# First-layer weights in column halves, the second half prepared during the second batch

## The chip, the core and the metric

The kernel runs on one core of a Trainium2 chip. The core has five engines with separate instruction streams: TensorE (PE, matrix products; its weight loads are listed as PEld), VectorE (DVE), ScalarE (ACT), GpSimd (POOL) and SyncE (SP), which here only issues DMA transfers. Each engine works through its own instructions in the order in which they were written and stops at the first whose inputs or buffers are not ready. The metric is the device time of one execution in microseconds (us).

## The reference

Attention over 8 batches of 8 heads, 576 positions and 64 channels, in which every score that lies more than tau below the maximum of its row is dropped, followed by two dense layers over all 4608 tokens. The numbers are float32 outside the kernel.

```python
scores = scale * np.matmul(q, k.transpose(0, 1, 3, 2))
thresh = np.max(scores, axis=-1, keepdims=True) - tau
scores = np.where(scores >= thresh, scores, -1000000000.0)
attn = softmax(scores)                     # written out in the reference
x = (attn @ v), heads side by side         # 4608 x 512
h = x @ w_in                               # 512 x 2048
out = (h - np.tanh(h)) @ w_out             # 2048 x 512
```

`w_in` and `w_out` hold 4 MB each in float32; the kernel keeps both in on-chip memory as bfloat16 (`w_in_sb`, `w_out_sb`).

## The kernel before

**Tiles.** Two heads form a pair; there are 32 pairs, four to a batch. A pair has nine tiles of 128 query rows: four for each head, and one that the last 64 rows of both heads share. That makes 288 tiles. The tile's scores are a 128 x 576 block (`psS`), written by PE from `kT` and `kS` (the pair's keys, transposed, and the same with halves swapped) and `qT`.

**What a pair needs first.** `load` brings k, q and v from memory over SP's queue (`kraw`, `qraw`, `vraw`). `split` on POOL makes a high and a low float16 part of k and of q (L184, L187, L188: three instructions each). `turn` transposes them, on PE with a copy by DVE (L258), or for the queries of every second pair from pair 9 on with a DMA transpose (L247); for keys POOL then makes `kS` (L264, two instructions). `split_v` on POOL casts the values (L216, L220, L221).

**A tile's way.** PE makes the scores; DVE scales them and takes their row maxima (L336, `sc`); once for two tiles DVE makes the threshold `nb` (L348); ACT applies the cut (`kink`, L363, giving `z`); `z` is transposed, for pairs 0 to 5 on PE (L382), from pair 6 on by a DMA transpose for two tiles at a time (L370, `zT`), issued on SP; ACT takes the exponential (`weights`, L391 after PE, L399 after the DMA, both giving `pT`); PE multiplies with the values (`attend`, L420, L427, L438); DVE divides (`norm`).

**The dense layers.** When a batch's four pairs are done, its 512 main tokens go through both layers in small steps put between the tiles of the next batch: `hidden` (L493, one of 16 column blocks of `w_in_sb`), tanh on ACT (L506), the subtraction on DVE (L512), `project` (L519, with `w_out_sb`). The last batch's share and the remaining rows run after the last tile.

**The order of work** is written out by hand. The main loop runs over s from -8; in step s the scores of tile s + 8 are made. I number steps by that tile, t = s + 8. So pair p's first scores come in step 9p. `PREP` and `plan` say in which step a pair's preparations are issued: `split` of k in step 9p - 8 and of q in 9p - 7 (for the odd pairs from 9 on in 9p - 10 and 9p - 9), the keys' `turn` in 9p - 5 (from pair 5 on in 9p - 6 or 9p - 3), `split_v` in 9p - 4, the loads in 9p - 16 to 9p - 14. In a tile's step t, ACT does the cut of tile t - 3, and the exponential of tile t - 4 in the first batch and of tile t - 8 later.

**The weights** come in 16 pieces of 512 KB, eight of `w_in` and then eight of `w_out`. A piece is loaded by SP into one of two float32 buffers `wt` (L638 for `w_in`, L634 for `w_out`), and POOL casts it into its place (L626). `w_when` lists the steps. In each listed step, after everything else of that step, the piece loaded at the previous listed step is cast and the next one is loaded. So SP stops at a load until POOL has cast the piece but one before it, and everything behind the load in SP's queue stops with it. Before, the loads stand in steps 3, 7, ..., 63 and the casts in steps 7, 11, ..., 67. A piece of `w_in` covers 128 of its 512 rows and half of its 2048 columns, pieces 0 and 1 being the left and the right half of the first rows, and so on.

The first `hidden` step stands in t = 49, the first that reads the right half of the columns (block 8) in t = 63, and the first that reads `w_out_sb` (L519) in t = 76.

Of the kernel before, what the change touches and what calls it, by code (L numbers as in the profile page):

```python
# [18 lines left out]
def kernel(  # L19
# [594 lines left out]
    def w_pieces():  # L614
        for w, sb, n in ((moe_w_in, w_in_sb, DM_C), (moe_w_out, w_out_sb, DF_C)):
            flat = sb.rearrange("p c n -> p (c n)")
            cols = n * w.shape[1] // 8
            src = w.rearrange("(c p) n -> p c n", p=P)
            for i in range(8):
                yield flat, src, i, cols, w.shape[1]  # L620

    loaded = []
# [50 lines left out]
    for t in ("k", "q", "v"):  # L673
        load(1, t)
    pieces = w_pieces()
    w_when = [4 * i + 3 for i in range(17)]

    todo, stage = [], 0
    fold = const.tile([P, 64], BF16, name="fold")
# [125 lines left out]
```

## Time and profile before

| | before |
|---|---|
| median of six runs | 534.15 us (533.56 to 535.31) |
| the profiled execution's own time | 534.04 us |
| its span in the profile | 532.1 us, so 1.9 us lie around it |
| PE busy | 505.9 us (95%) |
| DVE, ACT, POOL busy | 423.8, 436.2, 290.2 us |
| one cast of a weight piece (L626, POOL) | 1.039 us, 16 of them |
| one load of a weight piece, issue to landing | 4.5 us (`w_in`), 4.3 us (`w_out`) in the median |
| one DMA transpose of `z`, issue to landing | 3.6 us in the median, 6.3 us at most |

Times in the profile count from the start of the span. A line of the timeline gives start and duration, the engine, the line of the code, the operation with output <- input, and in brackets how long the engine stood idle before it and what ended that. In the rows by stretch each engine's busy time and its number of instructions are followed by the granted clock of PE, the mean busy share of the 16 DMA engines and the rate that they moved. The busy share of an engine over the whole span says little here: the first 60 us, with attention alone, are limited by other things than the 400 us in which both parts run side by side.

### The profile page before, as it was taken

What the parts mean: (1) busy time and instruction counts of PE and PEld (TensorE: products, weight loads), DVE (VectorE), ACT (ScalarE), POOL (GpSimd) and SP (SyncE); (2) the same over time, 40 slices, a digit from 0 to 9 for tenths busy, and PEclk for the clock granted to TensorE, in tenths of its full rate; (3) what the DMA queues carried; (4) which work ended last, traced back from release to release, by engine and by line L of the source; (5) the groups of instructions that cost most, each with busy time, mean ns of one, the idle gap of its engine ahead of it and who ended that gap; (6) DMA issues with size and microseconds to landing.
All of it is one profiled execution on the core that took longest, in us unless ns stands there. A gap on an engine that the chain in (4) does not pass through costs nothing.

```text
span 532.1 us, 12733 instructions
## 1 busy us (share of the span) xinstructions
PE 505.9 (95%) x4584; PEld 289.2 (54%) x4651; DVE 423.8 (80%) x1184; ACT 436.2 (82%) x617; POOL 290.2 (55%) x390
## 2 busy tenths in 40 slices
PE   8988899999999999999999999999999999999997
PEld 4666566554556565555555555655555555444444
DVE  5888878988988998898889998899889887554440
ACT  5999899998898998989888989898889899543330
POOL 7999987774745757475737574575747530000000
PEclk9999999999999999999999999999999999999999
DMA  7554557989997999899897999899989985401113
GB/s 212 176 187 147 173 160 193 186 167 187 171 201 148 190 179 211 173 169 211 188 186 156 198 187 194 147 193 186 205 169 177 200 155 110 105 22 39 39 41 79
DMA packets 202686, 85.31 MB, mean 160 GB/s; under 512 B 170240, under 2 KB 195072, under 8 KB 202624
## 3 DMA queue, kind: packets, MB, share of 16 engines
q1 hardware_dynamic: 202032, 84.08, 74.6%
q8 instruction: 36, 0.59, 0.4%
q10 hardware_dynamic: 592, 0.43, 0.3%
q14 instruction: 26, 0.21, 0.1%
HBM read 36.70 MB, written 9.44 MB: 87 GB/s over the span
## 4 chain that ended last, share of the span: by engine, by line
PE 63%; ACT 11%; POOL 8%; DVE 7%; issue 6%; DMA 4%; SPq 1%; POOLq 0%; ACTq 0%; DVEq 0%
PE psY L519 20%; PE psH L493 16%; PE psS L326 14%; ACT z L363 5%; PE psO L427 3%; ACT pT L399 3%; DMA zT<-z 3%; PE psHt L493 3%; ACT th L506 2%; POOL kS L264 2%; PE ps_k L235 2%; PE psS L317 2%; DVE sc L336 2%; DVE g L512 2%; POOL w_in_sb L626 1%
## 5 line engine op out<-in xcount | busy, mean ns | idle before, releaser
L336 DVE TENSOR_SCALAR_CACHE_REDUCE sc<-psS 128x576 f32<-128x576 f32 x288 | 214.4, 753 | 36.3 <-PE psS L326 22.7
L363 ACT ACTIVATE z<-sc,nb 128x576 bf16<-128x576 f32 x288 | 217.0, 771 | 29.1 <-DVE nb L348 27.1
L519 PE MATMUL psY<-w_out_sb,g 128*128 128x512 bf16 (+1 forms) x571 | 141.7, 373 | 2.4 <-issue 0.8
L264 POOL COPY kS<-kT 64x1152 f16<-64x1152 f16 x62 | 70.9, 1144 | 124.2 <-DVE nb L348 122.6
L399 ACT ACTIVATE pT<-zT 128x1152 f16<-128x1152 bf16 x117 | 135.1, 1155 | 3.8 <-DMA zT<-z 3.8
L493 PE MATMUL psH<-xT,w_in_sb 128*128 128x512 bf16 x436 | 114.1, 379 | 4.4 <-DVE g L512 2.3
L326 PE MATMUL psS<-kT,qT 128*128 128x512 f16 (+1 forms) x512 | 104.3, 285 | 4.6 <-DVE sc L336 2.0
L326 PEld LDWEIGHTS <-qT 128*128 128x128 f16 x1024 | 74.4, 97 | 59.9 <-issue 6.4
L512 DVE SCALAR_TENSOR_TENSOR g<-th,psH 128x512 bf16<-128x512 f32 x128 | 87.5, 684 | 21.3 <-ACT th L506 20.9
L326 PE MATMUL psS<-kS,qT 128*128 128x512 f16 x496 | 101.3, 286 | 0.3 <-POOL kS L264 0.3
L506 ACT ACTIVATE th<-psH 128x512 f32<-128x512 f32 x128 | 74.8, 584 | 23.3 <-PE psH L493 22.8
L519 PEld LDWEIGHTS <-g 128*128 128x128 bf16 x592 | 51.0, 98 | 56.8 <-issue 2.4
L493 PEld LDWEIGHTS <-w_in_sb 128*128 128x128 bf16 x576 | 49.1, 98 | 57.0 <-issue 4.7
L427 PE MATMUL psO<-vb,pT 128*128 128x65 bf16 x1024 | 53.3, 194 | 0.0
L427 PEld LDWEIGHTS <-pT 128*128 128x128 f16 x1024 | 44.2, 98 | 9.4
L188 POOL TENSOR_TENSOR qhl<-qraw,qhl 128x576 f16<-128x576 f32 x31 | 39.7, 1281 | 2.6
L188 POOL TENSOR_TENSOR khl<-kraw,khl 128x576 f16<-128x576 f32 x31 | 39.7, 1281 | 2.6
L391 ACT ACTIVATE pT<-psZ 128x512 f16<-128x512 bf16 (+1 forms) x54 | 35.0, 653 | 5.4 <-PE psZ L382 5.2
L532 DVE COPY yo<-psY 128x512 f32<-128x512 f32 (+1 forms) x31 | 21.1, 682 | 14.1 <-PE psY L519 12.4
L420 PE MATMUL psO<-vb,pT 128*128 128x130 bf16 x128 | 28.2, 221 | 1.4 <-ACT pT L399 0.6
L453 DVE TENSOR_TENSOR osb<-psO,rc 128x256 bf16<-128x256 f32 x64 | 27.2, 425 | 2.2
L258 DVE COPY kT<-ps_k 128x1152 f16<-128x1152 f16 x31 | 23.3, 753 | 5.8 <-PE ps_k L235 5.8
(79 smaller groups left out, 517.9 us busy)
## 6 DMA issues: line engine op xcount, KB each, us to landing
vraw<-in_v_dram SPq DMA_DIRECT2D x32, 256.0 KB, 3.8
out_dram<-yo SPq DMA_DIRECT2D x32, 256.0 KB, 3.0
kraw<-in_k_dram SPq DMA_DIRECT2D x31, 256.0 KB, 3.3
qraw<-in_q_dram SPq DMA_DIRECT2D x31, 256.0 KB, 3.6
wt<-in_moe_w_in_dram SPq DMA_DIRECT2D x8, 512.0 KB, 4.5
wt<-in_moe_w_out_dram SPq DMA_DIRECT2D x8, 512.0 KB, 4.3
zT<-z SPq DMA_TRANSPOSE x117, 3.6
kraw<-in_k_dram SPq DMA_DIRECT2D x32, 32.0 KB, 3.2
```

Of the source, the lines that this page charges most:

```text
L188: nc.gpsimd.tensor_tensor(out=hl[:, :, 1, :], in0=x, in1=hl[:, :, 0, :], op=ALU.subtract)
L264: nc.gpsimd.tensor_copy(out=o, in_=i)
L326: nc.tensor.matmul(out=ps[:, dst], lhsT=lhs, rhs=kk[:, src], start=(n == 0), stop=(n == 1),)
L336: nc.vector.tensor_scalar(out=sc, in0=ps[:, lo : lo + S], scalar1=SC, scalar2=None, op0=ALU.mult, op1=ALU.max, accum_out=mx[:, c : c + 1],)
L363: nc.scalar.activation(out=z, in_=sc, func=ACT.Prelu, bias=nb, scale=1.0, alpha=STEEP)
L391: nc.scalar.activation(out=pt[:, off * P : (off + n) * P], in_=ps[:, 0 : n * P], func=ACT.Exp)
L399: nc.scalar.activation(out=pt[:, 0 : n * P], in_=zts.pop(i)[:, 0:n, :], func=ACT.Exp)
L427: nc.tensor.matmul(out=po[:, t - 1 + ab, :], lhsT=pt[:, blk * P : (blk + 1) * P], rhs=vb[:, hh, c, :], start=False, stop=(n == 7), skip_gr ...
L493: nc.tensor.matmul(out=ps, lhsT=w_in_sb[:, c, n * P : (n + 1) * P], rhs=xs[m][:, c, :] if m < B else xR[:, c, :, :], start=(c == 0), stop= ...
L506: nc.scalar.activation(out=th, in_=ps, func=ACT.Tanh)
L512: nc.vector.scalar_tensor_tensor(out=gs[m][:, n, :], in0=th, scalar=-1.0, in1=ps, op0=ALU.mult, op1=ALU.add,)
L519: nc.tensor.matmul(out=ps, lhsT=gs[m][:, n, ms * P : (ms + 1) * P], rhs=w_out_sb[:, n, cols], start=(n == 0), stop=(n == DF_C - 1),)
```

## The change

The eight pieces of `w_in` come in another order, first the four left halves of the columns, then the four right halves. And `w_when` has other steps: the loads stand in steps 3, 11, 19, 27, then 32, 36, 40, 44 (the right halves), then 47, 50, 53, 56, 59, 62, 65, 68 (`w_out`). Each cast stands at the next listed step, so the casts are in 11, 19, 27, 32, 36, 40, 44, 47 for `w_in` and in 50, 53, 56, 59, 62, 65, 68, 71 for `w_out`. The number of pieces, their sizes and the instructions for each stay the same.

```diff
@@ -616,7 +616,8 @@
             flat = sb.rearrange("p c n -> p (c n)")
             cols = n * w.shape[1] // 8
             src = w.rearrange("(c p) n -> p c n", p=P)
-            for i in range(8):
+
+            for i in (0, 2, 4, 6, 1, 3, 5, 7) if w is moe_w_in else range(8):
                 yield flat, src, i, cols, w.shape[1]
 
     loaded = []
@@ -673,7 +674,7 @@
     for t in ("k", "q", "v"):
         load(1, t)
     pieces = w_pieces()
-    w_when = [4 * i + 3 for i in range(17)]
+    w_when = [3, 11, 19, 27] + [4 * i + 32 for i in range(4)] + [3 * i + 47 for i in range(9)]
 
     todo, stage = [], 0
     fold = const.tile([P, 64], BF16, name="fold")
```

## The prediction

> **What bounds the kernel now.** I read the 40 slices of the page (13.3 us each) first, then the chain that ended last, then the timelines of the engines in the two stretches that the change touches.
>
> ```profile
> ACT  5999899998898998989888989898889899543330
> POOL 7999987774745757475737574575747530000000
> DMA  7554557989997999899897999899989985401113
> ```
>
> POOL is at 9 only in slices 2 to 5; later it has room. The DMA engines are the other way round: 4 to 5 in slices 3 to 5, then 7 to 9 to the end of attention. The change moves POOL and DMA work from the first stretch into the beginning of the second.
>
> First stretch. In the chain everything from 15.7 to 57.8 us is POOL. But PE, the engine that uses POOL's work, waits little for it; its timeline has two such places worth something:
>
> ```profile
> 38.10 0.68 PE L235 MATMUL ps_q<-ident_f,qhl 128*128 128x128 f16 x9 [0.77 <-POOL qhl L188]
> ...
> 57.81 0.68 PE L235 MATMUL ps_k<-ident_f,khl 128*128 128x128 f16 x9 [0.41 <-POOL khl L188]
> ```
>
> A third, 0.40 us for `kS` at 18.05, lies before the first cast. Just after the wait at 38.10 ACT shows how close behind POOL it is: it runs without a gap from 30.6 to 38.95 and then loses only
>
> ```profile
> 39.58 0.70 ACT L391 ACTIVATE pT<-psZ 128x640 f16<-128x640 bf16 x1 [0.50 <-PE psZ L382]
> ```
>
> So POOL is first by a little; ACT is second.
>
> Second stretch, steps 64 to 79. ACT waits here twice for a transposed `z`, and both waits are in the chain:
>
> ```profile
> 103.30 6.08 DMA zT<-z
> ...
> 119.89 4.74 DMA zT<-z
> ```
> ```profile
> 109.46 1.16 ACT L399 ACTIVATE pT<-zT 128x1152 f16<-128x1152 bf16 x1 [0.64 <-DMA zT<-z]
> ...
> 124.74 1.17 ACT L399 ACTIVATE pT<-zT 128x1152 f16<-128x1152 bf16 x1 [1.76 <-DMA zT<-z]
> ```
>
> Counting the L399 rows from the first (tile 55), these are tiles 65 and 75. Why they are late is in SP's timeline. SP issues without a pause from 95.58 to 104.6, so `zT` of tile 65 goes out at 103.30 although its `z` was done at 101.7. And it does so again from 112.79:
>
> ```profile
> 112.79 1.29 SPq L247 DMA_TRANSPOSE qT<-qhl  x1
> 114.13 0.73 SPq L145 DMA_DIRECT2D kraw<-in_k_dram  x1
> ...
> 119.89 5.41 SPq L370 DMA_TRANSPOSE zT<-z  x3
> ```
>
> The transpose of pair 9's queries at 112.79 needs the POOL instruction that ended at 112.4 (L188 on `qhl`). Behind it SP spends 7.1 us on issues before `zT` of tile 75. So a late `split` on POOL delays ACT here. The DMA engines are full at the same time:
>
> ```profile
> 96.00:100.00 4.00, 3.63 (x42) 2.23 (x40) 3.60 (x12) 4.00 (x8) 3.85 (x5) 1.00 0.98 231
> 100.00:104.00 4.00, 3.95 (x40) 2.35 (x38) 3.96 (x12) 3.94 (x6) 1.24 (x4) 1.00 0.88 185
> 104.00:108.00 4.00, 3.44 (x36) 2.09 (x36) 3.78 (x10) 4.00 (x7) 3.26 (x4) 1.00 1.51 171
> ```
>
> From 130 to 220 us PE is busy 9.57 to 9.95 us in every 10, so what is lost or won before stays.
>
> **What the skill says.** The Trainium skill, "DMA: Bandwidth & Descriptors", section "Queues, rings and completion order", has descriptors on each DMA engine consumed in ring order, so a 512 KB load ahead of a transpose on SP's queue delays it. The trace fits: a transpose lands after 3.6 us in the median, but after 6.08 us behind q and v loads at 103.30. The same page, "Anatomy of one DMA", gives some 2 us of a transfer as fixed, so only part of a load's 4.3 us occupies the engines; I work that part out below. "GPSIMD Engine Reference", "Engine selection", calls one-input operations on POOL roughly line-rate; the trace has 1.039 us for a cast of 1024 columns, and all casts are alike, so column halves change no price.
>
> **The change, step by step.** Number and kind of instructions stay: 16 casts (16 x 1.04 = 16.6 us of POOL) and 16 loads. The tuple of piece numbers costs nothing on the chip. Only places change.
>
> *1. POOL relieved up to step 46.* Before the keys' split of pairs 2, 3, 4, 5, 6 and 7 there were 1, 3, 6, 8, 10 and 12 casts; now 0, 1, 3, 5, 7 and 10. POOL is thus 1.0 to 3.1 us earlier. Both PE waits go. At 38.10 PE was ready at 37.33, but the next scores need a buffer whose reader on DVE ended at 38.13, and they started at 38.61: 0.4 us won, which fits ACT's gap of 0.50. At 57.81 nothing else is in the way (the DVE copy behind it stood 0.99 us idle): 0.41 won. Together **-0.8 us**; not more than 0.77 + 0.41 = 1.2, and not under 0.4, if ACT swallows one of the two. SP, whose loads had waited 25 us for casts in this stretch, is freer too; nobody waited for those loads.
>
> *2. POOL fuller in steps 47 to 62.* Between the splits of pairs 6, 7 and 8, POOL has 5.45 (splits) + 2.40 (`kS`) + 1.27 (values) + 3 x 1.04 = 12.2 us of work. These periods last 12.8 and 14.65 us now, with idle of 1.79, 0.57 and 1.89 us. A cast now stands ahead of `kS` of pairs 6 and 7, where POOL waited for DVE's `kT`: with step 1's head start of 2 us it is done before. **0**; without that cover 1.0 each. The right halves are cast by step 47 and first read in step 63; `w_out` is first read in step 76.
>
> *3. Two more loads on a full queue.* Loads in steps 56, 59 and 62 stand about where 55, 59 and 63 stood. New are those in 65 (between the k load of pair 9 and `zT` of tile 63) and 68 (just behind `zT` of tile 65). Each costs SP an issue: 0.53 us at 88.25, 1.36 at 93.22. On the DMA engines: 211 GB/s at a share of 0.66 between 10 and 20 us make 320 at full share, so 524 KB take 1.6 us. `zT` of tile 65 is later by 0.5 (SP alone) to 1.6 us (no bubble in the queue); I take 1.0. Against that stand the 0.8 won: ACT's start of tile 65 moves by **+0.2** (-0.3 to +0.8). Tile 67 gets both loads; its exponential comes 3.4 us later with no wait in the trace, so I count nothing for it.
>
> *4. The last cast.* It stood at 99.11, before POOL's 3.27 us of idle: free. Now it is in step 71, behind pair 9's split of k and ahead of that of q, which SP's transpose waits for. POOL's chain there starts with `kT` of pair 8 and is 0.8 earlier: q's split ends at 112.4 - 0.8 + 1.04 = 112.65 if the piece has landed. It is issued behind `zT` of tile 65, at about 104.5; with 4.3 (median) to 5.4 us (longest `w_out` load) it lands at 108.8 to 109.9. POOL is ready at 109.7 - 0.8 = 108.9. So q's split ends 0.25 to 1.25 us later than before; I take 0.6. Behind it are queued the query transpose, the loads of k, q and v, `zT` of tiles 73 and 75, and with that ACT at 124.74, for which PE waited 1.1 us: **+0.6 us** against now.
>
> *Sum.* The steps meet at ACT's tile 75, and the latest counts: step 4. The span goes from 532.1 to 532.7, the profiled execution from 534.04 to 534.65. The median of the runs lies 0.1 above the latter: **534.7 us**. The 0.8 us of step 1 is given back, and a little more. A measurement of this kernel tells about 0.2%, 1.07 us, from no change.
>
> **Rivals.**
>
> *The gain is kept (faster).* The two DMA waits hang on how transposes and other transfers meet: flights from 3.2 to 6.3 us stand in the trace. If tile 75's flight falls from 4.74 to the median 3.6, 1.1 us more comes off, and step 1 shows: 534.15 - 0.8 = 533.3, with 1.76 us of waiting gone at best 531.6. For it: both long flights may be chance. Against: the added cast and issues are certain.
>
> *The last piece lands late (slower).* If wt of step 68 flies as long as the longest transfer here, 6.3 us, and SP reaches it at 104.9, it lands at 111.2; cast to 112.2, q's split to 114.95, 2.5 us later than before. SP stands behind it, ACT's tile 75 too: 536.6. It decides once the landing is later than 108.9 + 1.1 = 110.0, where the loss passes 0.2%. For it: DMA shares of 0.9 to 1.5 there. Against: 5.4 us is the longest of the eight.
>
> *No effect.* ACT bounds the first batch alone, and the second stretch absorbs the loads: 534.1.
>
> **Numbers.** Chances: given back 0.40 (nearly all of it within 0.2%), kept 0.27 (0.20 faster by more than 0.2%), late piece 0.28, no effect 0.05. That makes faster 0.20, within 0.2% 0.46, slower 0.34. The range is 532.6 to 536.4: the upper end takes most of the late piece, the lower leaves out the case in which both waits go. The likeliest case's own range is 533.8 to 535.4.
>
> **What would show it.** Step 1: no wait for POOL at PE's two transposes, and `ps_k` of pair 5 at about 57.0. Step 2: POOL idle before `kS` of pairs 6 and 7. Step 3: `wt` issues among the `zT` issues of 97 to 105, and over 0.64 us of ACT's wait at tile 65. Step 4: the last cast between two splits, and the query transpose later than 112.79. I am wrong if the first batch gains over 1.2 us, or if ACT's waits for `zT` shrink.

## The result

| | before | changed |
|---|---|---|
| median | 534.05 us (38 runs) | 536.17 us (17 runs) |
| lowest to highest | 532.97 to 536.27 | 534.28 to 539.43 |
| profiled execution: span | 532.1 us | 535.9 us |

The ratio is 1.0048, 95% interval 1.0037 to 1.0059: slower by 2.1 us in the median, where I had forecast 0.6. The profiled execution is one of the longer ones (537.7 us).

The slices of the page, first two rows of the kernel before, then three of the changed kernel:

```profile
PE   8988899999999999999999999999999999999997
PEclk9999999999999999999999999999999999999999
```
```profile
PE   7988899996999999999999999999999999999997
POOL 7998987873665757275727575575747540000000
PEclk9999999997999999999999999999999999999999
```

POOL is less full in slices 4 to 8, as intended. PE falls from 9 to 6 in slice 10 (121 to 134 us), and with it the clock granted to PE falls to 7, which stood at 9 in every slice before. In this execution all of the loss is there.

The first batch did what step 1 said. PE's transpose of pair 5's keys has no wait on POOL, and ACT's gap, 0.50 us before, is 0.15 (timelines of PE and ACT):

```profile
57.21 0.66 PE L235 MATMUL ps_k<-ident_f,khl 128*128 128x128 f16 x9
```
```profile
39.55 0.70 ACT L391 ACTIVATE pT<-psZ 128x640 f16<-128x640 bf16 x1 [0.15 <-PE psZ L382]
```

That is 0.60 us earlier than before (57.81), although this execution had begun 0.31 us later (ACT's first cut at 10.72 against 10.41): 0.9 us won.

It is lost again behind the last cast. First two lines of the kernel before, the end of its split of q (POOL) and its transpose of `z` of tile 73 (SP):

```profile
111.19 1.28 POOL L188 TENSOR_TENSOR qhl<-qraw,qhl 128x576 f16<-128x576 f32 x1
```
```profile
116.80 1.65 SPq L370 DMA_TRANSPOSE zT<-z  x1
```

POOL's timeline of the changed kernel (its lines from 619 on stand one lower than before), between the splits of pair 9's k (first line) and q (last):

```profile
107.91 1.28 POOL L188 TENSOR_TENSOR khl<-kraw,khl 128x576 f16<-128x576 f32 x1
110.75 1.04 POOL L627 CAST w_out_sb<-wt 128x1024 bf16<-128x1024 f32 x1 [1.55 <-DMA wt<-in_moe_w_out_dram]
...
113.24 1.28 POOL L188 TENSOR_TENSOR qhl<-qraw,qhl 128x576 f16<-128x576 f32 x1
```

The cast waits 1.55 us for its piece, and q's split ends at 114.5, 2.0 us later than before. SP stands until then:

```profile
104.80 0.53 SPq L635 DMA_DIRECT2D wt<-in_moe_w_out_dram  x1
...
114.55 1.28 SPq L247 DMA_TRANSPOSE qT<-qhl  x1
...
118.38 1.78 SPq L370 DMA_TRANSPOSE zT<-z  x1
```

The last piece was issued at 104.80 and landed 5.9 us later, just before its cast. Behind the query transpose come the loads of k and q and then, at 118.38, `zT` of tile 73; before it went out at 116.80. ACT and PE:

```profile
123.64 1.16 ACT L399 ACTIVATE pT<-zT 128x1152 f16<-128x1152 bf16 x1 [4.36 <-DMA zT<-z]
```
```profile
124.85 0.29 PE L420 MATMUL psO<-vb,pT 128*128 128x130 bf16 x1 [4.30 <-ACT pT L399]
```

Tile 73's exponential had no wait in the kernel before:

```profile
120.48 1.17 ACT L399 ACTIVATE pT<-zT 128x1152 f16<-128x1152 bf16 x1
```

PE stops for 4.3 us, and the stretches of 2 us (busy time of PE, PEld, DVE, ACT, POOL, then the granted clock) show the clock at half after it:

```profile
120.00:122.00 2.00, 0.55 (x4) 0.12 (x2) 1.82 (x6) 0.00 (x0) 1.91 (x2) 1.00 1.35 85
122.00:124.00 2.00, 0.00 (x0) 0.00 (x0) 0.00 (x0) 0.36 (x1) 1.25 (x3) 0.91 1.03 265
124.00:126.00 2.00, 1.15 (x15) 1.15 (x16) 0.00 (x0) 2.00 (x3) 1.92 (x4) 0.50 1.22 258
126.00:128.00 2.00, 1.78 (x8) 0.72 (x7) 1.39 (x5) 2.00 (x4) 0.56 (x3) 0.50 0.74 135
128.00:130.00 2.00, 2.00 (x8) 0.81 (x7) 0.18 (x1) 1.75 (x3) 0.00 (x0) 0.50 1.04 216
130.00:132.00 2.00, 2.00 (x19) 1.07 (x18) 1.55 (x4) 1.08 (x2) 0.00 (x0) 0.88 0.87 177
```

By tile 81's exponential the changed kernel is 3.7 us behind (137.06 against 133.34), and 3.8 at the end of the span. The wait of 4.36 us is not all of that, and not all of it counts. The kernel before waits 1.76 us for `zT` of tile 75, where the changed kernel does not wait any more, and at that tile it is only 1.3 us behind (126.04 against 124.74). Another 2.4 us come from there to tile 81, a stretch of work that takes 11.02 us instead of 8.60 and in which PE's clock is at half up to about 130.5.

A second profile of the changed kernel comes from an execution nearer the median (536.20 us). ACT waits 3.08 us at tile 73 and then once more:

```profile
126.16 1.16 ACT L399 ACTIVATE pT<-zT 128x1152 f16<-128x1152 bf16 x1 [1.29 <-DMA zT<-z]
```

This execution is 1.4 us behind the kernel before at tile 75 and still 1.4 at tile 81; the rest of its 2.3 us comes at waits for `zT` of tiles 111 and 263. So 1.3 to 1.4 us by tile 75 are common to both profiles, and what comes behind differs.

### The profile page after: what moved, and what is told of

It reads as the page before. It is cut to its first block, busy times and chain, and to the rows that moved or that the text cites. A ratio compares the mean times of both kernels' runs of the same rounds, so it can differ in the third digit from the quotient of the medians.

```text
span 535.9 us, 12739 instructions
## 1 busy us (share of the span) xinstructions
PE 506.9 (95%) x4584; PEld 290.1 (54%) x4651; DVE 423.8 (79%) x1184; ACT 436.4 (81%) x617; POOL 290.4 (54%) x390
## 4 chain that ended last, share of the span: by engine, by line
PE 67%; ACT 11%; DVE 9%; issue 6%; POOL 4%; DMA 2%; SPq 0%; ACTq 0%; POOLq 0%; DVEq 0%
PE psY L519 20%; PE psH L493 16%; PE psS L326 15%; ACT z L363 5%; PE psO L427 4%; DVE sc L336 3%; ACT pT L399 3%; PE psHt L493 3%; ACT pT L391 2%; DVE g L512 2%; PE ps_k L235 2%; PE psS L317 2%; DMA zT<-z 2%; ACT th L506 1%; PE psO L438 1%
## 5 line engine op out<-in xcount | busy, mean ns | idle before, releaser
L493 PE MATMUL psH<-xT,w_in_sb 128*128 128x512 bf16 x436 | 114.8, 381 | 4.5 <-DVE g L512 2.3
L493 PEld LDWEIGHTS <-w_in_sb 128*128 128x128 bf16 x576 | 49.3, 98 | 57.4 <-issue 5.5
```

Of the source, the lines that this page charges most:

```text
L493: nc.tensor.matmul(out=ps, lhsT=w_in_sb[:, c, n * P : (n + 1) * P], rhs=xs[m][:, c, :] if m < B else xR[:, c, :, :], start=(c == 0), stop= ...
```

## The experiments

Theory A: the last cast stands between two splits and waits for its piece; the lateness goes over the split of q and SP's query transpose to the transposes of z, and so to ACT and PE. Theory B: the two loads now issued in steps 65 and 68 make the transposes of z slow on the DMA engines themselves. Ratios are to the kernel before, run beside it on the same chip.

**The last cast behind q's split.**

```diff
-    w_when = [3, 11, 19, 27] + [4 * i + 32 for i in range(4)] + [3 * i + 47 for i in range(9)]
+    w_when = [3, 11, 19, 27] + [4 * i + 32 for i in range(4)] + [3 * i + 47 for i in range(8)] + [73]
```

> The changed kernel with one number changed: the last cast moves from step 71 to step 73, behind the split of pair 9's q. All loads, the late ones in steps 65 and 68 too, stay where they are. Theory A (the last cast, waiting on POOL for its piece, holds up the split of q, and with it SP's query transpose and the transposes of z behind it): the loss goes, about 533.4 us (532.8 to 534.2), ACT has no wait for zT over 2 us, and the mean granted clock is back at 0.998 or more. Theory B (the two late loads slow the transposes on the DMA engines): nothing changes, about 536.2 us, the long wait for zT stays.

Measured: 534.13 us (20 runs, 532.03 to 535.96), before 533.52; ratio 1.0005 (0.9992 to 1.0019). One number takes back nearly all of the loss, which speaks for A. But the median is 0.7 us above 533.4, and its profiled execution, one of the longest (535.92), has a wait still:

```profile
116.25 1.80 SPq L370 DMA_TRANSPOSE zT<-z  x1
```
```profile
121.74 1.16 ACT L399 ACTIVATE pT<-zT 128x1152 f16<-128x1152 bf16 x1 [2.69 <-DMA zT<-z]
```

SP is on time here, and the transpose takes 5.5 us to be used. Against theory A's expectation there is thus a wait over 2 us, and in nine of the 20 executions the mean clock is 0.996 or 0.997. So A is the larger part and not the whole.

**The late cast alone, in the kernel before.**

```diff
-    w_when = [4 * i + 3 for i in range(17)]
+    w_when = [4 * i + 3 for i in range(15)] + [68, 71]
```

> The kernel before with its last two listed steps moved from 63 and 67 to 68 and 71, so that the last piece is loaded in 68 and cast in 71, between the splits of pair 9's k and q; the 15 pieces ahead of it keep their steps up to 59. Theory A: the loss appears with this alone, 536 to 537.5 us, with a wait of ACT for zT of 3 us or more near 120 us and a dip of the granted clock behind it. Theory B (two more loads in the crowded stretch): only one load has moved, from 63 to 68, and the number of loads in steps 56 to 72 is as before, so 534.0 to 534.8 us.

Measured: 536.86 us (4 runs, 536.24 to 537.11); ratio 1.0059 (1.0044 to 1.0074). In its trace POOL's cast waits 1.33 us for its piece, the query transpose is issued at 114.93, and

```profile
124.22 1.16 ACT L399 ACTIVATE pT<-zT 128x1152 f16<-128x1152 bf16 x1 [4.33 <-DMA zT<-z]
```

One load and two casts moved make the whole loss, without any of the rest of the change. B had no more than 534.8 for it.

**The query transpose behind the transpose of z.** The changed kernel with SP's order of two transposes exchanged; POOL is as late as before.

```diff
-        d = 7 if q_by_dma(p) else 3 - (p == 1 or p % 2 == 0 or p >= 5)
+        d = (5 if p == 9 else 7) if q_by_dma(p) else 3 - (p == 1 or p % 2 == 0 or p >= 5)
```

> The changed kernel with one number changed: SP's DMA transpose of pair 9's queries is issued in step 76, behind the transpose of z of tile 73, and no longer in step 74 ahead of it. POOL's order, the casts and the weight loads stay, so q's split is as late as in the changed kernel. Theory A (POOL's lateness reaches ACT over SP, which stands at the query transpose and keeps the transposes of z waiting): ACT's wait near 120 us falls under 1.5 us and the time to 532.5 to 534 us. Theory B (the two late loads make the transposes of z slow on the DMA engines): the wait and the time stay as in the changed kernel of the same call.

Measured: 532.80 us (22 runs), before 533.79; ratio 0.9982 (0.9971 to 0.9992), where the changed kernel beside it had 1.0051. ACT has no wait for `zT` of tile 73, although q's split ends at 115.1, later still than in the changed kernel. With q's split on time the same exchange wins nothing (0.9977 against 0.9980, below), so what it wins here is POOL's lateness: it is SP's queue that carries it to ACT. What is late next is the queries themselves:

```profile
120.64 0.44 PE L317 MATMUL psS<-kT,qT 128*64 128x512 f16 x4 [2.16 <-DMA qT<-qhl]
```

**A third buffer, so that the cast does not wait.** The casts stay in their steps; each load goes one listed step earlier.

```diff
-    wt_pool = pool("wt", 2)
+    wt_pool = pool("wt", 3)
...
                 if piece:
                     w_load(piece)
+                if s + AHEAD == 3:
+                    w_load(next(pieces))
```

> The changed kernel with three buffers for the weight pieces and each load one listed step earlier (two in step 3, the last in step 65); the casts stay in their steps, the last between the splits of pair 9's k and q. So the cast is there, but it doesn't wait for its piece. If the cast's own 1.04 us is what counts: q's split is 1 us late, 535 us or more. If the wait for the landing (1.5 us in the profile) is needed as well: q's split ends about 0.3 us later than in the kernel before, 533 to 534.5 us. Theory B: one load fewer among the transposes behind step 65, between the two, 535 us.

Measured: 534.16 us (22 runs); ratio 1.0013 (1.0003 to 1.0022). The cast, now at 108.94 without a wait, lets q's split end at 112.7, 0.2 us later than in the kernel before, as worked out. Of the loss of 0.51% that the changed kernel had beside it, 0.38 went with the wait for the piece. The last load moved from step 68 to 65 with it, so a share of that may be the load's place. ACT's wait at tile 73 did not go, since this transpose, issued at 116.60, took 5.3 us to land:

```profile
122.04 1.16 ACT L399 ACTIVATE pT<-zT 128x1152 f16<-128x1152 bf16 x1 [2.95 <-DMA zT<-z]
```

But at tile 75 this execution is 0.3 us ahead of the kernel before: the wait stands in the place of the 1.76 us there.

**All loads done by step 62.**

```diff
-    w_when = [3, 11, 19, 27] + [4 * i + 32 for i in range(4)] + [3 * i + 47 for i in range(9)]
+    w_when = [3, 11, 19, 27] + [4 * i + 32 for i in range(4)] + [47, 49, 51, 53, 55, 57, 59, 62, 67]
```

> The changed kernel with the pieces of w_out closer together: loads in steps 47, 49, 51, 53, 55, 57, 59, 62 and the last cast in 67, where the kernel before had it; the first layer's part as in the changed kernel. Both theories: the loss goes and the gain of the first batch shows, 533.4 us (532.8 to 534.0). If it is not faster than before, the gain of the first batch (0.8 us worked out) isn't carried to the end.

Measured: 532.90 us (12 runs), ratio 0.9991 (0.9980 to 1.0001). On another chip:

> The version whose loads are done by step 62 once more, for the same chip: 0.5 to 0.8 us under the kernel before.

Measured: 532.99 us (22 runs), before 534.00; ratio 0.9980 (0.9972 to 0.9987). So 0.5 to 1.0 us are won: the two profiles are 0.8 us ahead at tile 63, the first batch's gain, and 2.0 and 1.4 us at tile 75, where they have no wait for `zT` left. Against the kernel with the last cast in 73, which has loads in 65 and 68 (1.0005, run beside the first of the two), the first ratio is 0.14% less, 0.7 us. The intervals overlap, so that is all that can be put down to theory B, and even that is not shown.

**Is the slow clock part of the loss?** The changed kernel again, and then with 60 products of zeros on PE while it waits (run twice, first on another chip, then on the same):

> The changed kernel itself, for the same chip: 2 us over the kernel before, with a granted clock of 0.993 to 0.998 by the execution.

Measured: 536.36 us (6 runs), ratio 1.0051 (1.0034 to 1.0068).

```diff
         po = ops[p, hh]
+        if i == 73:
+            for _ in range(60):
+                nc.tensor.matmul(
+                    out=fulls[p, hh][:, 392:504], lhsT=zero[:, 0:P], rhs=zero[:, 0:112],
+                    start=True, stop=True, skip_group_check=True,
+                )
```

(The lines that take the accumulator `psO` 512 columns wide for this are left out.)

> The changed kernel with 60 extra products of 128 x 112 zeros on PE ahead of the first product of tile 73, written into an unused part of the same accumulator: about 3 us of work in a stretch where PE only waits for tile 73's exponential. Theory A with the clock (the stop of PE of 4.3 us lets its clock fall to half for some 6 us, and this makes most of the loss): granted clock near 1.00 throughout, the long wait for zT still there, 534.5 to 535.5 us. Without the clock (the wait alone makes the loss, or the slow clock costs nothing): 536 us or more.

Measured, on the other chip: 535.87 us (8 runs); ratio 1.0046 (1.0031 to 1.0060), between the two expectations.

> The changed kernel with the 60 products of zeros once more, to be set against the changed kernel on the same chip. If the slow clock behind the stop is a part of the loss: clock 1.00 and a median at least 0.8 us under that of the changed kernel, though the zeros' 3 us are a floor for the stop. If it costs nothing: the same median or a higher one.

Measured, on the same chip as the changed kernel: 536.45 us (5 runs); ratio 1.0053 (1.0040 to 1.0066). The clock stayed at 0.999 or 1.000 in all 13 executions, against 0.994 to 0.997 in the changed kernel, but the median did not fall: what I expected of the slow clock failed. In the second profile the zeros did not hold PE up:

```profile
120.81 3.12 PE L423 MATMUL psO<-zero 128*128 128x112 bf16 x60
124.95 0.23 PE L428 MATMUL psO<-vb,pT 128*128 128x130 bf16 x1 [1.02 <-ACT pT L399]
```

But the medians can't decide it. Both profiles of this version have a wait at tile 219 that no other profile has, and lose 0.72 and 0.94 us by it (L501 is L493 of the changed kernel; the second profile):

```profile
356.83 1.16 ACT L399 ACTIVATE pT<-zT 128x1152 f16<-128x1152 bf16 x1 [0.84 <-PE psH L501]
```

The version with the zeros thus has a cost of its own, whose cause I don't know, and which can hide a gain of this size. Single traces do show a difference in pace. From tile 75's exponential to tile 81's it takes 8.60 us in the kernel before and in both profiles with the zeros. Where the clock fell to half it takes 11.02 and 8.61 us (the two profiles of the changed kernel), 9.56 (last cast in 73) and 9.64 (the late cast alone): between nothing and 2.4 us more. The stops themselves vary by more than a microsecond from trace to trace (ACT's wait: 4.36 and 3.08 us in the changed kernel, 3.23 and 4.08 with the zeros). So whether the slow clock costs anything in the median stays open.

**A version that beats both.** SP's queue behind the query transpose was crowded in the kernel before too. In the version with early loads I moved the three loads of pair 10 behind the transposes of z:

```diff
         for d, f in PREP[3 if p == 1 else 0 :]:
-            d -= p == 1 and d in (3, 5)
+            d -= 3 * (p == 10 and d >= LDK - 2) + (p == 1 and d in (3, 5))
```

> The version whose loads are done by step 62 (last cast in 67), and in it the three loads of pair 10 (k, q, v) three steps later, in 77 to 79, so that SP issues the transposes of z of tiles 73 and 75 ahead of them. Theory A says that the wait of 1.1 us for zT of tile 73 left in that version comes from SP's queue behind the query transpose: it goes, 0.5 to 1.3 us under that version, about 532.0 us. If the wait is the flight of the transpose itself: no difference to that version.

Measured: 531.74 us (6 runs, 531.17 to 532.27), before 534.00; ratio 0.9953 (0.9941 to 0.9966), 1.25 us under the version without this edit. `zT` of tile 73 goes out at 113.57 and that of tile 75 at 116.42, and ACT has no wait for either.

> The version whose loads are done by step 62, and in it the query transpose of pair 9 behind the transpose of z of tile 73 (step 76). Theory A: as with the loads of pair 10 later, about 532.0 to 532.6 us, unless PE now waits for the queries, as it did for 2.2 us where q's split was late; here that split ends 3 us earlier, so a wait under 1 us.

Measured: 532.79 us (22 runs), ratio 0.9977 (0.9970 to 0.9984): no better than without the edit (0.9980). PE waits 1.60 us for the queries, more than I had allowed; the wait has only changed its place.

> The kernel before, unchanged in its weights, with the three loads of pair 10 three steps later (77 to 79). Theory A: the wait of 1.76 us for zT of tile 75, which stood behind these loads on SP, was in the kernel before already and goes, so 532.3 to 533.3 us; the rest of what the best version won (2.3 us) is the first batch's. If the best version's gain needs the moved weights: 533.7 us or more.

Measured: 532.15 us (5 runs), before 533.82; ratio 0.9966 (0.9952 to 0.9979). So 0.34% lay in the kernel before and needs no weight moved; the moved weights of the first batch add about 0.13%, by ratios from two chips whose intervals overlap.

## Why the prediction was wrong

*Step 1* held: 0.8 us worked out, 0.9 measured.

*Step 2* held: POOL stood idle before `kS` of pairs 6 and 7 (1.11 and 0.51 us) with the casts ahead of them.

*Step 3* had the place wrong. Tile 65's exponential was to come 0.2 us later; it came at 108.11 instead of 109.46, with no wait in the profile. That long flight before was one of the flights that vary. The loads in 65 and 68 cost about 0.7 us in all by the runs, with intervals that overlap; I had taken 1.0.

*Step 4* is the one that failed, by its sizes; the mechanism is the one measured. I let the last piece land between 108.8 and 109.9, from flights of 4.3 to 5.4 us, and took 0.6 us for q's split. It landed after 5.9 us, longer than any of the eight before, POOL waited 1.55 us, and q's split was 2.0 us late. Eight flights from other places gave no upper bound for a load put among transposes.

Then I let the lateness arrive at tile 75, because there the trace had a wait. It arrived at tile 73. That one had no wait before, which I read as slack, but it had none: issued at 116.80 and used at 120.48, 3.7 us, just the median flight of 3.6. Of the wait of 4.36 us the later issue is 1.6, the longer flight (5.2 us against 3.6) another 1.6, and 1.2 is that ACT itself was ready earlier (119.28). At tile 75, where step 4 had put +0.6 us, the changed kernel's two profiles are 1.3 and 1.4 us late. What is missing from there to the median's 2.1 us came behind it, in one profile beside the slow clock and in the other at later transposes, and step 4 had nothing for it.

The flight was partly luck. In the ten profiles in which this transpose goes out behind both the query transpose and the loads of k and q it took 3.6 to 5.4 us to land, and the 3.6 of the kernel before is the shortest; in the two in which it goes out ahead of these loads it took 3.3 and 3.7. So a load ahead of it on the queue often goes with a longer flight, as the prediction had it, but not always.

Two figures of step 4 and of its rival were read or added wrongly. The 1.1 us that "PE waited" at tile 75 are the wait of its weight load; PE itself stood idle for 0.62. And as a landing at 108.9 costs 0.25 us already, a loss of 0.2% (1.07 us) begins with a landing at 109.7 and not at 110.0.

The rival "the last piece lands late" is what happened. Its point of decision was passed by either figure, with a landing at 110.7. I had given it 0.28, against 0.40 for the landing in time. Its price of 536.6 us is 0.4 off the median, but partly by luck, since it put 2.5 us on tile 75, where 1.3 and 1.4 were measured. The median lies inside the range, near its upper end; the forecast of no change beyond 0.2% was wrong.

What I left out altogether is the granted clock. Whether it costs time is not settled by the experiment with the zeros.

## What to carry to other kernels

Work moved out of a busy stretch lands in an order somewhere else: what counts there is not the engine's free time but what stands behind the moved instruction. A cast that waits for a DMA is a wait put in front of everything after it on that engine, and here it went from POOL over one transpose in SP's queue to ACT and PE. And an operand that arrives without a wait may have no slack at all: compare issue to use with the usual flight, and with how far flights spread, before calling it hidden.

## What I had not expected of the hardware

After PE's stop of 4.3 us its granted clock was at half for about 6.8 us (0.91, three stretches at 0.50, and 0.88 in the stretches above; a stretch of 2 us at clock c holds 4 x (1 - c) us at half). It was for about 3.4 us after stops of 3.02 (the changed kernel's second profile), 2.69 (last cast in 73), 4.27 (the late cast alone) and 2.16 us (query transpose behind `z`), but a stop of 2.89 us (third buffer) left it at 1.00. So the length of the stop alone doesn't decide it. The mean clock goes with the time in the 18 executions of the changed kernel in the first comparison: 0.998 with 534.3 us, 0.996 or 0.997 with 535.4 to 536.6, 0.994 with 537.0 to 538.4, 0.993 with 539.4. In the six later ones it does so less closely: 534.8 us came with 0.996, and 536.5 and 536.7 with 0.994. The Trainium skill describes such a gate in "TensorE: Matmul & The Clock Gate", "Part 1: The HAM clock gate (the "warmup" mystery)", with a return to full speed after about 3.4 us of activity; the spells at half measured here are about one and two times that.
